# Layer 2 of the last five chunks by seven block products, and a written-out order for the last seven chunks

## The chip, the cores and the metric

The kernel runs on one core of one Trainium2 chip. The metric is device time in microseconds (us), the median of three runs. Engines: PE (matmuls), DVE, ACT and POOL (elementwise work), SP (issues nearly all DMAs).

## What is computed

Pooled attention, then a feed-forward block with a residual, on 8 batches x 576 tokens = 4608 tokens with 512 features:

```
k_p, v_p = mean of k, v over groups of 8 tokens          # 72 keys per batch, 8 heads of 64
attn = softmax(q @ k_p.T / 8);  x = attn @ v_p           # heads side by side: 4608 x 512
xn = (x - mean) / sqrt(var + 1e-6) * g_ln
out = x + max(xn @ w_ch1, 0) @ w_ch2                     # 512 -> 2048 -> 512
```

Inputs and output are float32. The kernel holds each factor of the feed-forward matmuls as a float16 main part and a float16 rest, and multiplies main x main, main x rest and rest x main: three matmuls for one product.

## The kernel before, in words

The tokens are cut into 36 tiles of 128 and 9 chunks of 512 (four tiles). Layer 1 gives for a chunk H = max(xn W1, 0), 2048 wide, in two halves (h = 0, 1) of 1024; layer 2 multiplies each half by its half of W2 and adds the result to x. Weights stay in SBUF as `wt[1]` and `wt[2]`, eight blocks each (and one spare), with main part and rest.

Layer 1 of chunks 2 to 8 works by seven products (Strassen's scheme in Winograd's form). The tokens of a chunk and the 512 features are cut in two each, and so are the features and the 1024 columns of a W1 half; seven products of blocks and of sums of blocks take the place of eight. `FACTOR` names them: A11, A12, A22 and S1 to S4 are blocks of z (the normalised x) and sums of them, B11, B21, B22 and T1 to T4 the same of W1. `product` (L807) runs six matmuls with 256 moving columns; `first_products`, `middle_products` and `last_product` bring the results from PSUM into a float32 buffer `cc` (ACT copies L835, L836, L842, L845; DVE additions L838, L844, L851), and then write H to `ring` as main part (ReLU on ACT, L857) and rest (DVE, L858). f = 0..3 counts the column blocks of a half: one f gives 2 x 128 columns of H for 512 tokens.

Layer 2, `ffn_out` (L870), is the plain product. For a half and a tile of 128 tokens it runs 24 matmuls with 512 moving columns (L882), weights from `ring`, moving columns from `wt[2]`. DVE adds the scaled result to x (L893), and after the second half SP writes the tile out (L898).

Attention for a later chunk runs between: `stage_a` (scores on PE L501, softmax on DVE, ACT and POOL L537, L540, then a DMA transpose L548) and `stage_b` (values on PE L633 and L634, statistics and z on DVE L681 and L698, the sums S1 to S4 L702 to L705, the split into main part on ACT L751 and rest on POOL L753, a DMA transpose L758). `prep_k` and `prep_v` load a batch's K and V and pool them on POOL (L371 to L375, L385 to L387).

Order of the work: chunks 0 and 1, all loading and preparing of weights, the sums T of W1 (`sums_w`, L339 to L347, L327) and attention up to tile 11 are written out by hand in the list START. A token names an operation, and each time it appears the operation goes on to its next `yield`; each engine gets its instructions in the order of the list. For chunks 2 to 8 the loop at the end of the kernel calls units one after the other, four of layer 1 and four of layer 2 for each half; `A_AT` and `B_AT` say before which unit a tile's attention stages stand, and a scheduler in the compiler then orders the instructions.

## Time and profile before

| what | value |
|---|---|
| median of three runs | 842.06 us (841.86 to 843.77) |
| the profiled execution | 842.33 us, its span 840.6 us |
| mean granted TensorE clock | 0.993 of full speed |
| PE, DVE, POOL, ACT busy | 96%, 65%, 41%, 40% of the span |
| first layer-1 product of chunk 2 | 242.9 us after the start of the span |
| last matmul ends | about 837 us |

How to read it: the span goes from the first to the last instruction of one execution; the time has about 2 us around it. "Busy" of PE is the union of its matmuls, which overlap one another, so the mean length of one (379 ns for 512 columns) is not what one costs in a row. In a group of instructions the columns are the source line, the engine, the operation, the output and inputs by their names, the shapes and the count, then busy us and mean ns, then how long the engine stood idle before them and for whom. A line of the chain gives its start, its length and the work in it.

### The profile page before, as it was taken

How to read it: one execution, taken by the hardware profiler on the slowest of the kernel's cores; microseconds unless marked ns; L12 is line 12 of the kernel's file. 1: busy time of each engine (PE TensorE's matmuls, PEld its weight loads, DVE VectorE, ACT ScalarE, POOL GpSimd, SP SyncE). 2: the span in 40 equal slices, each digit the busy share in tenths (PEclk: the TensorE clock that was granted, in tenths of full speed). 3: DMA queues.
4: the chain of work that ended last, by engine and by line, in shares of the span. 5: the costliest groups of instructions: out<-in, count | busy, mean ns of one | idle time of the engine just before them, and what ended most of it. 6: DMA issues, size and time to landing. Idle time of an engine off the chain costs nothing.

```text
span 840.6 us, 14847 instructions
## 1 busy us (share of the span) xinstructions
PE 809.4 (96%) x5742; PEld 527.5 (63%) x5742; DVE 545.3 (65%) x1110; ACT 339.1 (40%) x636; POOL 347.0 (41%) x497
## 2 busy tenths in 40 slices
...
GB/s 362 310 156 237 203 151 134 67 74 61 124 180 83 122 43 126 110 121 54 121 69 120 43 134 75 116 39 94 78 88 39 101 51 76 27 101 14 1 1 51
DMA packets 145975, 87.37 MB, mean 104 GB/s; under 512 B 125424, under 2 KB 126576, under 8 KB 143728
## 3 DMA queue, kind: packets, MB, share of 16 engines
...
q10 hardware_dynamic: 1152, 0.90, 0.5%
...
## 4 chain that ended last, share of the span: by engine, by line
PE 70%; DVE 10%; POOL 9%; DMA 4%; issue 3%; ACT 2%; ACTq 0%; SPq 0%; POOLq 0%; DVEq 0%
PE ps_f L882 34%; PE ps_f L817 25%; PE ps_f L784 5%; PE ps_a L501 3%; DMA vr<-in_v_dram 2%; POOL vr L385 2%; POOL vr L386 1%; DVE w L264 1%; POOL vp L387 1%; POOL kblk L375 1%; PE ps_m L441 1%; POOL pt L575 1%; PE ps_a L633 1%; DVE w L211 1%; PE ps_a L634 1%
## 5 line engine op out<-in xcount | busy, mean ns | idle before, releaser
L882 PE MATMUL ps_f<-w,ring 128*128 128x512 f16 x1728 | 380.7, 379 | 0.0
L882 PEld LDWEIGHTS <-ring 128*128 128x128 f16 x1728 | 167.7, 98 | 193.8 <-issue 0.2
L817 PE MATMUL ps_f<-zts,w 128*128 128x256 f16 x1680 | 209.0, 274 | 8.2 <-DVE rowmax L168 3.4
L817 PEld LDWEIGHTS <-w 128*128 128x128 f16 x1680 | 164.2, 98 | 30.1 <-issue 8.9
L893 DVE SCALAR_TENSOR_TENSOR x<-ps_f,cy,x 128x512 f32<-128x512 f32 x72 | 53.8, 748 | 114.4 <-PE ps_f L882 107.8
L537 POOL TENSOR_TENSOR phl<-e,phl 128x512 f16<-128x512 f32 x32 | 38.5, 1204 | 142.5 <-ACT phl L527 142.4
L817 PE MATMUL ps_f<-zts,tsp 128*128 128x256 f16 x672 | 96.1, 272 | 0.3 <-ACT raw L835 0.3
L784 PE MATMUL ps_f<-zts,w 128*128 128x512 f16 (+1 forms) x480 | 87.0, 340 | 3.2 <-DVE ring L795 2.4
L857 ACT ACTIVATE ring<-raw 128x512 f16<-128x512 f32 x112 | 64.8, 622 | 58.4 <-DVE raw L851 57.9
L858 DVE SCALAR_TENSOR_TENSOR ring<-raw,ring 128x512 f16<-128x512 f32 x112 | 81.6, 755 | 8.7 <-ACT ring L857 8.4
L835 ACT COPY raw<-ps_f 128x256 f32<-128x256 f32 x56 | 20.8, 371 | 138.2 <-PE ps_f L817 134.8
L753 POOL TENSOR_TENSOR hl<-raw,hl 128x640 f16<-128x640 f32 x28 | 41.4, 1495 | 81.4 <-ACT hl L751 45.6
L784 PEld LDWEIGHTS <-w 128*128 128x128 f16 x480 | 47.0, 99 | 40.0 <-issue 3.7
L817 PEld LDWEIGHTS <-tsp 128*128 128x128 f16 x672 | 64.0, 98 | 10.7 <-issue 0.5
L385 POOL TENSOR_TENSOR vr<-vr 72x256 f32<-72x256 f32 x56 | 50.0, 898 | 34.3 <-DMA vr<-in_v_dram 34.0
L851 DVE TENSOR_TENSOR raw<-ps_f,raw 128x256 f32<-128x256 f32 x112 | 42.3, 418 | 22.6 <-PE ps_f L817 22.6
L838 DVE TENSOR_TENSOR raw<-ps_f,raw 128x256 f32<-128x256 f32 x56 | 23.7, 424 | 48.4 <-PE ps_f L817 43.0
L844 DVE TENSOR_TENSOR raw<-ps_f,raw 128x256 f32<-128x256 f32 x56 | 23.5, 420 | 32.6 <-PE ps_f L817 27.4
L751 ACT CAST hl<-raw 128x640 f16<-128x640 f32 x28 | 19.2, 722 | 62.6 <-DVE a L728 26.3
L501 PE MATMUL ps_a<-kblk,q 128*128 128x144 f32 (+1 forms) x320 | 43.1, 288 | 0.9 <-DVE st L661 0.9
L501 PEld LDWEIGHTS ps_a<-kblk,q 128*128 128x128 f32 (+1 forms) x320 | 39.1, 179 | 6.4 <-issue 1.3
L753 POOL TENSOR_TENSOR hl<-z,hl 128x512 f16<-128x512 f32 x18 | 21.5, 1196 | 36.0 <-ACT hl L751 22.7
(144 smaller groups left out, 1002.9 us busy)
## 6 DMA issues: line engine op xcount, KB each, us to landing
...
```

The source lines that it names most:

```text
L385: eng.tensor_add(out=vr[:, 0:4, :], in0=vr[:, 0:4, :], in1=vr[:, 4:8, :])
L501: nc.tensor.matmul(ps[r, p // 2, p % 2 * 2 * KV : (p % 2 + 1) * 2 * KV], lhsT=q[:, p, r], rhs=kblk[b % NKB][:, p, :], start=True, stop=True,)
L537: nc.gpsimd.tensor_tensor(out=ph[:, 0, :, KA:P], in0=e[:, :, 0:KA], in1=ph[:, 0, :, 0:KA], op=ALU.subtract)
L753: nc.gpsimd.tensor_tensor(out=zhl[:, 1, :], in0=src, in1=zhl[:, 0, :], op=ALU.subtract)
L784: nc.tensor.matmul(ps, lhsT=w[:, part, fs], rhs=zT[:, kz, cols], start=(n == 0), stop=(n == 3 * NKT - 1),)
L817: nc.tensor.matmul(ps, lhsT=w[:, part, f * P : (f + 1) * P], rhs=z, start=start and n == 0, stop=stop and n == 3 * KH - 1, skip_group_chec ...
L838: nc.vector.tensor_tensor(out=cc[:, 0, :HC], in0=m2, in1=cc[:, 0, :HC], op=ALU.add)
L851: nc.vector.tensor_tensor(out=cc[:, j, HC:], in0=u3, in1=cc[:, j, HC:], op=ALU.add)
L857: nc.scalar.activation(out=hh[:, 0, f], in_=cc[:, j], func=AF.Relu)
L858: nc.vector.scalar_tensor_tensor(out=hh[:, 1, f], in0=cc[:, j], scalar=0.0, in1=hh[:, 0, f], op0=ALU.max, op1=ALU.subtract)
L882: nc.tensor.matmul(ps, lhsT=h[:, part, i, cols], rhs=w[:, wp, j], start=(n == 0), stop=(n == 3 * NFT // 2 - 1),)
L893: nc.vector.scalar_tensor_tensor(out=x, in0=ps, scalar=out_scale(c, tt, half), in1=x, op0=ALU.mult, op1=ALU.add)
```

## The change

Chunks 4 to 8 (c >= `C_TWO`) get layer 2 by seven products too. A half of H (512 tokens x 1024) is cut in two by tokens and in two by columns, the half of W2 (1024 x 512) in two by rows and by columns.

- *W2.* In chunks 2 and 3 `keep_w2` (KW) copies three blocks of each half of W2 to DRAM; `sums_w2` (TW, 16 steps) builds T1 to T4 in pieces of 128 columns (two DVE additions, four POOL subtractions, a split by ACT and POOL) and writes them to DRAM, two DMAs a step. From chunk 4 on `load_w2` (LW) reads one of the seven factors, 512 KB, for each product into one of four places in `ring`, which H no longer needs.
- *H.* `wt[2]` becomes the place of H's seven factors, one place each, and of the scratch `s_tmp`. For each f, EL makes A11 and A12 (ReLU and main part on ACT, rest on DVE), ER the ReLU of the other half of `cc` and A22, ES four sums on POOL, EP the split of S1 and S2 (i = 0) and of S3 and S4 (i = 1): main part on ACT, rest on POOL, for i = 0 in chunks 4 and 5 on DVE. `cc` has three buffers; the third is one of the two softmax buffers, which from tile 12 on is only one.
- *Products.* `out_seven` (O, c.h.n.u) runs 12 matmuls with 256 moving columns for one product n = 0..6 and one row tile u = 0, 1; three PSUM results per u gather them, and DVE adds each state that is final for a part of x into x. `W2_USE` gives the order n: A11, A12, A22, S1, S2, S4, S3.
- *Order.* The loop goes; STEADY, a list like START, orders every step of chunks 2 to 8. Layer 1 is `product` (P, c.h.f.m) with one eviction each, the seventh as one DVE instruction over 512 columns, and `whole_h` (WH) in chunks 2 and 3. z of chunks 3 to 8 is made on ACT.

The core of the diff:

```diff
+C_TWO = 4
-A_AT, B_AT = (0, 2, 5, 8), (4, 6, 11, 12)
+LO_GPSIMD = (6,7,8)
+STEADY = """
+P.2.0.0.2 TW.0.0.0 TW.0.0.0 A.12 HV.4.0 A.12 P.2.0.1.2 P.2.0.1.1 P.2.0.0.1 P.2.0.0.5 P.2.0.1.5 A.12 P.2.0.1.1 P.2.0.1.1
+P.2.0.0.1 P.2.0.0.1 A.12 A.12 TW.0.0.0 HV.4.0 HV.4.0 A.12 A.12 KW.1.1 KW.1.1 P.2.0.1.6 P.2.0.0.2 P.2.0.0.2 TW.0.0.1
...
+HV.7.1 HV.7.1 EP.6.0.3.1 EL.6.1.1 EP.6.0.3.1 EP.6.0.3.1 B.29 O.6.0.3.0 P.6.1.1.7 P.6.1.1.7 O.6.0.3.1 O.6.0.3.1
+O.6.0.3.0 O.6.0.3.0 EL.6.1.0 EL.6.1.0 B.30 O.6.0.4.1 O.6.0.4.1 ER.6.1.1 A.31 EP.6.1.0.0 A.31 ES.6.1.0 ES.6.1.0
+EP.6.1.0.0 EP.6.1.0.0 ES.6.1.1 A.31 A.31 B.29 B.29 O.6.0.5.1 O.6.0.6.0 O.6.0.6.1 P.6.1.2.1 O.6.0.5.1 O.6.0.5.1
+O.6.0.6.0 O.6.0.6.0 O.6.0.6.1 O.6.0.6.1 P.6.1.2.1 P.6.1.2.1 B.30 P.6.1.2.5 P.6.1.2.2 P.6.1.2.6 P.6.1.3.2 P.6.1.3.1
+P.6.1.2.2 P.6.1.2.2 B.30 B.30 P.6.1.2.5 P.6.1.2.5 O.6.0.5.0 P.6.1.2.4 B.31 O.6.0.5.0 O.6.0.5.0 B.31 P.6.1.2.6 P.6.1.2.6
+P.6.1.3.1 P.6.1.3.1 Z.30.0 EP.6.1.0.1 EP.6.1.1.0 P.6.1.2.4 P.6.1.2.4 EP.6.1.0.1 EP.6.1.0.1 ES.6.1.1 ES.6.1.1 Z.30.0
+Z.30.0 EP.6.1.1.0 EP.6.1.1.0 LW.6.1.1 LW.6.1.1 LW.6.1.0 LW.6.1.0 LW.6.1.2 LW.6.1.2 P.6.1.3.5 P.6.1.3.6 P.6.1.2.3
+P.6.1.2.3 P.6.1.2.3 P.6.1.3.2 P.6.1.3.2 P.6.1.3.5 P.6.1.3.5 Z.30.1 P.6.1.3.6 P.6.1.3.6 EP.6.1.1.1 EL.6.1.2 Z.30.1
...
-    ring = ctx.enter_context(tc.tile_pool(name="ring", bufs=2))
+    dram = ctx.enter_context(tc.tile_pool(name="dram", bufs=1, space=bass.MemoryType.DRAM))
...
+    ring = const.tile([P, 2, 2 * FPQ * CH], F16, name="ring")
...
-        ph = phl[t % 2]
+        ph = phl[t % 2 if t < 3 * TPC else 0]
...
-        (nc.gpsimd if c < 2 else nc.vector).tensor_scalar(
-            out=z, in0=x, scalar1=ln[:, 0:1], scalar2=ln[:, 2:3], op0=ALU.subtract, op1=ALU.mult
-        )
+        if c > 2:
+            nc.vector.scalar_tensor_tensor(
+                out=ln[:, 0:1], in0=ln[:, 0:1], scalar=-1.0, in1=ln[:, 2:3], op0=ALU.mult, op1=ALU.mult
+            )
+            yield
+            nc.scalar.activation(out=z, in_=x, func=AF.Identity, scale=ln[:, 2:3], bias=ln[:, 0:1])
+        else:
+            (nc.gpsimd if c < 2 else nc.vector).tensor_scalar(
+                out=z, in0=x, scalar1=ln[:, 0:1], scalar2=ln[:, 2:3], op0=ALU.subtract, op1=ALU.mult
+            )
         if not seven:
...
+    def left_buffer(c, h, f):
+        if "c" not in t_raw:
+            t_raw["c"] = t_raw.pop("t1").rearrange("p n c -> p (n c)").rearrange(
+                "p (i f c) -> p i f c", i=2, f=2
+            )
+        if c < C_TWO:
+            return t_raw["c"][:, f % 2]
+        if not C_BUF:
+            raw = phl[1].rearrange("p a h k -> p (a h k)").bitcast(F32).rearrange("p (i c) -> p i c", c=CH)
+            C_BUF.extend((t_raw["c"][:, 0], t_raw["c"][:, 1], raw))
+        return C_BUF[(2 * FPQ * c + FPQ * h + f) % 3]
+
+    def product(c, h, f, m):
+        if m in (1, 2, 5):
+            PS[c, h, f, m] = psum["ps_f"].tile([P, CH], F32, name="ps_f")
...
-                    start=start and n == 0,
-                    stop=stop and n == 3 * KH - 1,
+                    start=m in (1, 2, 4, 5) and n == 0,
+                    stop=m in (2, 3, 4, 7) and n == 3 * KH - 1,
...
+        j, k = divmod({1: 0, 2: 0, 3: 2, 4: 1, 5: 3, 6: 2, 7: 1}[m], 2)
+        o = cc[:, j, k * HC : (k + 1) * HC]
+        if m in (2, 3):
+            nc.vector.tensor_tensor(out=o, in0=ps, in1=o, op=ALU.add)
+        elif m == 7:
+            o = cc[:, :, HC:]
+            nc.vector.tensor_tensor(out=o, in0=ps.unsqueeze(1).broadcast_to([P, 2, HC]), in1=o, op=ALU.add)
+        else:
+            nc.scalar.copy(out=o, in_=ps)
...
+    def split_h(src, n, f, engine):
+        hi, lo = (wt[2][:, n, a, f * HC : (f + 1) * HC] for a in range(2))
+        nc.scalar.copy(out=hi, in_=src)
+        yield
+        engine.tensor_tensor(out=lo, in0=src, in1=hi, op=ALU.subtract)
+
+    def left_factors(c, h, f):
+        cc = left_buffer(c, h, f)[:, :, :HC]
+        nc.scalar.activation(out=cc, in_=cc, func=AF.Relu)
+        yield from split_h(cc, slice(0, 2), f, nc.vector)
+
+    def right_relu(c, h, f):
+        cc = left_buffer(c, h, f)
+        nc.scalar.activation(out=cc[:, :, HC:], in_=cc[:, :, HC:], func=AF.Relu)
+        yield from split_h(cc[:, 1:2, HC:], slice(2, 3), f, nc.vector)
+
+    s_tmp = wt[2][:, WB - 1].rearrange("p a n -> p (a n)").bitcast(F32).rearrange("p (i c) -> p i c", c=HC)
+
+    def right_sums(c, h, f):
+        cc = left_buffer(c, h, f)
+        r00, r01, r10, r11 = (cc[:, j, k * HC : (k + 1) * HC] for j in range(2) for k in range(2))
+        nc.gpsimd.tensor_tensor(out=s_tmp[:, 0], in0=r01, in1=r11, op=ALU.add)
+        nc.gpsimd.tensor_tensor(out=s_tmp[:, 1], in0=s_tmp[:, 0], in1=r00, op=ALU.subtract)
+        yield
+        nc.gpsimd.tensor_tensor(out=s_tmp[:, 3], in0=r10, in1=s_tmp[:, 1], op=ALU.subtract)
+        nc.gpsimd.tensor_tensor(out=s_tmp[:, 2], in0=r00, in1=r01, op=ALU.subtract)
+
+    def right_pair(c, h, f, i):
+        yield from split_h(s_tmp[:, 2 * i : 2 * i + 2], slice(3 + 2 * i, 5 + 2 * i), f, nc.gpsimd if i or c in LO_GPSIMD else nc.vector)
+
+    w2s = [dram.tile([7, P, FPQ // FPB, 2, FPB, HC], F16, name=f"w2s{h}") for h in range(2)]
+
+    def keep_w2(h, n):
+        i, j = ((0, 0), (1, 0), (1, 1))[n]
+        src = wt[2][:, 4 * h + 2 * i : 4 * h + 2 * i + 2].rearrange("p b a n -> p (b a n)")
+        src = src.rearrange("p (g n) -> p g n", n=CH)[:, :, j * HC : (j + 1) * HC]
+        nc.sync.dma_start(out=w2s[h][n].rearrange("p b a f n -> p (b a f) n"), in_=src)
+
+    def sums_w2(h, f, e):
+        flat = phl[1].rearrange("p a h k -> p (a h k)")
+        b = wk2.tile([P, POOL, KV], F32, name="kr").rearrange("p l k -> p (l k)")[:, : 4 * P]
+        b = b.rearrange("p (i c) -> p i c", c=P)
+        t = flat[:, e * 8 * P : (e + 1) * 8 * P].rearrange("p (i a c) -> p i a c", i=4, a=2)
+        for i in range(2):
+            src = wt[2][:, 4 * h + 2 * i + f // 2].rearrange("p a (f j c) -> p a f j c", f=FPB, j=4)[:, :, f % 2]
+            nc.vector.tensor_tensor(
+                out=b[:, 2 * i : 2 * i + 2], in0=src[:, 0, e::2], in1=src[:, 1, e::2], op=ALU.add
+            )
+        yield
+        b11, b12, b21, b22 = (b[:, i] for i in range(4))
+        nc.gpsimd.tensor_tensor(out=b11, in0=b12, in1=b11, op=ALU.subtract)
+        nc.gpsimd.tensor_tensor(out=b12, in0=b22, in1=b12, op=ALU.subtract)
+        yield
+        nc.gpsimd.tensor_tensor(out=b22, in0=b22, in1=b11, op=ALU.subtract)
+        nc.gpsimd.tensor_tensor(out=b21, in0=b21, in1=b22, op=ALU.subtract)
+        yield
+        nc.scalar.copy(out=t[:, :, 0], in_=b)
+        yield
+        nc.gpsimd.tensor_tensor(out=t[:, :, 1], in0=b, in1=t[:, :, 0], op=ALU.subtract)
+        yield
+        for a in range(2):
+            dst = w2s[h][W2_AT["T1"] : W2_AT["T1"] + 4, :, f // FPB, a, f % FPB, e * P : (e + 1) * P]
+            nc.sync.dma_start(out=dst.rearrange("i p c -> p i c"), in_=t[:, :, a])
+
+    W2_USE = (("A11", "B11"), ("A12", "B21"), ("A22", "T4"), ("S1", "T1"), ("S2", "T2"), ("S4", "B22"), ("S3", "T3"))
+    W2_AT = {n: i for i, n in enumerate(("B11", "B21", "B22", "T1", "T3", "T4", "T2"))}
+    H_AT = {n: i for i, n in enumerate(("A11", "A12", "A22", "S1", "S2", "S3", "S4"))}
+
+    def w2_buffer(c, h, n):
+        return ring.rearrange("p i (j b a f c) -> p (i j) b a f c", j=2, a=2, f=FPB, c=HC)[:, (14 * c + 7 * h + n) % 4]
+
+    def load_w2(c, h, n):
+        nc.sync.dma_start(out=w2_buffer(c, h, n), in_=w2s[h][W2_AT[W2_USE[n][1]]])
+
+    PO = {}
+
+    def out_seven(c, h, n, u):
+        left, b = H_AT[W2_USE[n][0]], w2_buffer(c, h, n)
+        if n in (0, 1, 3):
+            PO[c, h, u, n] = psum["ps_f"].tile([P, CH], F32, name="ps_f")
+        ps = PO[c, h, u, {0: 0, 1: 1, 2: 1, 3: 3, 4: 0, 5: 3, 6: 0}[n]][:, :HC]
+        for f in range(FPQ):
+            for part, wp in ((0, 0), (0, 1), (1, 0)):
+                nc.tensor.matmul(
+                    ps,
+                    lhsT=wt[2][:, left, part, f * HC + u * P : f * HC + (u + 1) * P],
+                    rhs=b[:, f // FPB, wp, f % FPB],
+                    start=n < 4 and f == 0 and part == wp == 0,
+                    stop=f == FPQ - 1 and part == 1,
+                    skip_group_check=True,
+                )
+        yield
+        tt = u + 2 * (n in (2, 3, 6))
+        t = c * TPC + tt
+        x, scale = X[t], out_scale(c, tt, h)
+        if n == 6:
+            x = x.rearrange("p (j c) -> p j c", j=2)
+            ps = ps.unsqueeze(1).broadcast_to([P, 2, HC])
+        else:
+            x = x[:, HC:] if n in (3, 4, 5) else x[:, :HC]
+        nc.vector.scalar_tensor_tensor(out=x, in0=ps, scalar=scale, in1=x, op0=ALU.mult, op1=ALU.add)
+        if h == 1 and n in (5, 6):
+            yield
+            nc.sync.dma_start(out=out[t * P : (t + 1) * P, :], in_=X.pop(t))
 
...
+    def run(tokens):
+        begun = {}
+        with tc.manual_schedule():
+            for token in tokens.split():
+                if token not in begun:
+                    name, *args = token.split(".")
+                    begun[token] = iter(ops[name](*map(int, args)) or ())
+                next(begun[token], None)
+            for steps in begun.values():
...
+    run(START)
...
-    for c in range(2, NRUN):
...
-            all_of(op(*args))
+    run(STEADY)
```

368 lines of the change are left out of this document (293 added, 75 removed).

## The prediction

> **What bounds the kernel now.** I read the page's first part, then the windows cut at the first layer-1 product of each chunk (chunk 2 starts at 242.9 us, chunk 8 ends at 837.0), then the chain in order of time, then the groups by form.
>
> ```profile
> PE 809.4 (96%) x5742; PEld 527.5 (63%) x5742; DVE 545.3 (65%) x1110; ACT 339.1 (40%) x636; POOL 347.0 (41%) x497
> ```
>
> ```profile
> 242.90:330.20 87.30, 85.12 (x627) 57.15 (x627) 53.48 (x122) 30.16 (x64) 44.43 (x79) 0.98 0.45 106
> 330.20:417.20 87.00, 84.37 (x628) 57.89 (x627) 54.78 (x123) 31.44 (x67) 36.43 (x60) 1.00 0.44 99
> 417.20:503.50 86.30, 86.30 (x658) 58.84 (x657) 56.58 (x119) 31.59 (x67) 31.89 (x51) 1.00 0.37 92
> 503.50:589.60 86.10, 83.78 (x621) 56.99 (x619) 55.39 (x122) 31.17 (x67) 23.34 (x37) 1.00 0.37 85
> 589.60:674.60 85.00, 85.00 (x651) 57.97 (x650) 52.33 (x112) 30.70 (x66) 15.39 (x18) 1.00 0.32 72
> 674.60:758.76 84.16, 84.16 (x627) 57.77 (x626) 52.31 (x112) 30.67 (x66) 13.95 (x14) 1.00 0.32 64
> 758.76:837.00 78.24, 78.12 (x528) 51.41 (x526) 28.92 (x57) 20.24 (x48) 0.00 (x0) 1.00 0.04 14
> 837.00:840.60 3.60, 0.00 (x0) 0.00 (x0) 0.67 (x1) 0.00 (x0) 0.00 (x0) 0.90 0.19 73
> ```
>
> The columns behind the length are busy us of PE, weight loads, DVE, ACT and POOL, then granted clock, DMA share and GB/s. In chunks 2 to 8 (one row each) PE is busy 586.85 of 594.10 us: it is the bound, at full clock, with 7.25 us of idle to win. DVE stands at 61 to 66% until chunk 7, ACT at 35 to 37%, and POOL falls from 51% to 17%. Busy time alone does not say that PE works at its best rate, so I take rates from unbroken runs on the chain:
>
> ```profile
> 174.16 20.72 PE ps_f L882 x96
> 758.76 16.38 PE ps_f L817 x150
> 779.47 18.35 PE ps_f L882 x85
> 836.91 0.75 DVE x L893
> ```
>
> 96 matmuls with 512 moving columns take 20.72 us, 215.8 ns each; 150 with 256 columns take 16.38, 109.2 ns each. The narrow form costs 0.506 of the wide one.
>
> **The change part by part.** *Layer 2 of chunks 4 to 8.* Before, a chunk has 2 halves x 4 token tiles x 24 = 192 wide matmuls: 41.43 us. After, it has 2 halves x 7 products x 2 row tiles x 12 = 336 narrow ones: 36.69 us. That is 4.74 us a chunk, **23.7 us** for five, all on the path. Layer 1, attention and layer 2 of chunks 2 and 3 keep their matmuls.
>
> [...]
>
> *The floor.* The first 242.9 us keep their list, and the load of the first stage changes nothing but where a buffer lies. 242.9 + 586.85 - 23.7 = 806.05; with the 3.60 us behind the last matmul and the 842.33 - 840.60 = 1.73 us that the profiled execution has beside its span, a PE without any idle gives 811.4. (Its 842.33 is 0.27 above the median of 842.06, well inside the 0.3%, 2.5 us, that can be told from no change here.)
>
> *What a fixed list leaves idle.* The stage before is run from such a list already:
>
> ```profile
> 120.00:160.00 40.00, 40.00 (x209) 19.59 (x207) 30.05 (x52) 16.37 (x25) 33.93 (x37) 1.00 0.48 121
> 160.00:200.00 40.00, 40.00 (x187) 18.16 (x186) 25.05 (x39) 9.69 (x17) 31.43 (x45) 1.00 0.22 54
> 200.00:242.90 42.90, 41.55 (x267) 21.54 (x265) 33.86 (x76) 14.93 (x25) 25.78 (x39) 1.00 0.52 124
> ```
>
> PE idles 1.35 of 122.9 us, 1.1%, beside a POOL that is 74% busy. On 563 us that is 6.2 us; it takes the place of the 7.25.
>
> *The new elementwise work,* by these rows:
>
> ```profile
> L858 DVE SCALAR_TENSOR_TENSOR ring<-raw,ring 128x512 f16<-128x512 f32 x112 | 81.6, 755 | 8.7 <-ACT ring L857 8.4
> L857 ACT ACTIVATE ring<-raw 128x512 f16<-128x512 f32 x112 | 64.8, 622 | 58.4 <-DVE raw L851 57.9
> L893 DVE SCALAR_TENSOR_TENSOR x<-ps_f,cy,x 128x512 f32<-128x512 f32 x72 | 53.8, 748 | 114.4 <-PE ps_f L882 107.8 <-PE ps_m L191 3.9 <-PE ps_f L191 1.8
> L838 DVE TENSOR_TENSOR raw<-ps_f,raw 128x256 f32<-128x256 f32 x56 | 23.7, 424 | 48.4 <-PE ps_f L817 43.0 <-ACT raw L835 5.1
> L753 POOL TENSOR_TENSOR hl<-raw,hl 128x640 f16<-128x640 f32 x28 | 41.4, 1495 | 81.4 <-ACT hl L751 45.6 <-issue 35.9
> L339 DVE TENSOR_TENSOR raw<-w 128x512 f32<-128x512 f16 x16 | 15.4, 1018 | 0.0
> ```
>
> ```profile
> L385 POOL TENSOR_TENSOR vr<-vr x56: 714/723/1782, 28.5 to 505.3; 72x256 f32<-72x256 f32 x56
> L753 POOL TENSOR_TENSOR hl<-raw,hl x28: 1390/1400/1851, 227.0 to 750.3; 128x640 f16<-128x640 f32 x28
> L753 POOL TENSOR_TENSOR hl<-z,hl x18: 1148/1155/1905, 119.7 to 711.1; 128x512 f16<-128x512 f32 x18
> L341 POOL TENSOR_TENSOR raw<-raw x4: 1274/1646/1652, 120.8 to 186.7; 128x512 f32<-128x512 f32 x4
> ```
>
> For each of a chunk's 8 column blocks of H:
> - ACT loses two splits (L857) and gains two ReLUs, the A11/A12 split, the half-width A22 split and two splits of sums: about 5.4 instructions for 2, +3.4 x 0.62 = 2.1 us. It also makes the normalised z, six instructions of about 0.62. Per chunk +17 +4 = 21 us: ACT at 52 of 80. If the new Identity function needs a table of its own, two loads at 1.28 each of the six times are 15 us, which the 28 left still cover:
>
> ```profile
> L446 ACT ACT_TABLE_LOAD x1 | 1.3, 1283 | 0.8 <-PEq L1029 0.8
> ```
>
> - DVE loses L858 twice (1.4) and gains rests of 0.7 and 0.42 (in chunks 4 and 5 another 0.7). Each half has 12 evictions at 0.42 and two at 0.75 where four at 0.75 were: +7.1 a chunk, while z leaves it (about -3). DVE lands near 54 to 62 of 80.
> - POOL gains four sums at 0.72 (L385) and one rest at 1.16 (L753; two in chunks 6 to 8): 4.0 or 5.2 us, 32 or 42 a chunk. Chunk 4: 31.9 + 32 = 64 of 80, chunk 7: 14 + 42 = 56.
> - Chunks 2 and 3 get 8 steps each of W2 sums: DVE 2 x 0.5 (half of L339), four POOL sums of 128 columns, at most 0.72 each, a split: 4.0 us of POOL, 32 a chunk. Chunk 2: 44.4 + 32 = 76 of 84.5, the fullest stage of any engine but PE. Nobody but the later loads waits for these sums.
>
> Attention and K/V steps keep their instructions and engines (K/V of batch 4 in chunk 2, of 7 until chunk 6), so their shares stand in the rows already. By sums all of this lies beside PE and costs nothing. By order it need not: H's parts have one place each, so POOL may start the S parts of a half only behind the last layer-2 product of the half before, and PE needs them all before its S4 and S3 products. In chunk 6 the list has for PE between those two points ten layer-2 products (12 x 109.2 = 1.31 us, 13.1), ten layer-1 products (6.6) and three attention steps (about 3.0: chunk 7's 84.16 less 78.12 is 6.0 for eight): 22.7 us. For POOL it has seven rests (8.1), five half steps of sums (7.2), four z rests of 640 columns (5.6): 20.9, and the first waits for an ACT split of 0.62. Slack 1 us in 22.7. Counted likewise the second halves of chunks 4, 5, 7, 8 have 0, 3, 0 and 5 us, first halves 2 to 16 (chunk 4's, at the turn from the old scheme, is 4 short unless some of it runs early). L753's mean stands 7% over its median where others do not get in its way: 7% of some 22 us is 1.5 us a half, minus what slack there is. I put **4 us** for the nine boundaries: 0 if the medians hold, 14 if every half loses its 1.5.
>
> [...]
>
> *Loads.* 70 loads of 512 KB come in, in SP's queue, with the transposes and q loads behind each one that waits for its slot; the waiting one holds back attention's transposes, two tiles ahead of their use. Rows:
>
> ```profile
> 0.00:40.00 40.00, 29.64 (x230) 22.65 (x230) 29.20 (x53) 25.63 (x33) 19.02 (x31) 1.00 0.94 351
> ```
>
> ```profile
> 502.53 2.66 DMA vr<-in_v_dram
> ```
>
> At 351 GB/s a load takes 1.5 us of all 16 engines, 14 a chunk 21 us: DMA share 0.37 + 0.26. 144 KB landed 2.66 us after issue; 368 KB more at that rate make 3.7, as an estimate, between 2.7 and, behind another load, 5.2. The tightest is the fifth of each half: its slot is free when the first product has run, and it is used two to three products of 2.6 us later, 4.9 us in chunk 6. It fits at 3.7; at 5.2 it costs 0.3 us in ten halves, 3 us. I take 0. The W2 sums leave in 256-byte runs in chunks 2 and 3 and are read tens of us later: nothing, or 2 us once if the first load comes too early.
>
> *Tail.* Four outputs of 256 KB instead of one follow in the last 5 us: 0.75 MB at 351 GB/s is 2.1 us more, partly under the last products: +1.
>
> Sum: 811.4 + 6.2 + 4 + 1 = 822.6, say **822**.
>
> **The rivals.** *POOL sets the end (slower).* The price of a POOL instruction decides. L341's row shows 1646 where 1274 was possible, a factor of 1.29. At that factor the windows, of 15 to 42 us of POOL work, overrun PE by 8, 3, 6, 6 and 0 us in the second halves and by 16, 3, 8, 4 and 0 in the first: 54 us, and 811.4 + 54 + 1 = 866. It turns slower from a factor of about 1.19, where the overruns make 30. For it: no slack in three halves. Against it: medians at the minima while DVE ran at 65%, and a cheap change of engine:
>
> ```profile
> 809.63 1.15 ACT L857 ACTIVATE ring<-raw 128x512 f16<-128x512 f32 x2 [1.58 <-DVE raw L851]
> 810.29 1.29 DVE L858 SCALAR_TENSOR_TENSOR ring<-raw,ring 128x512 f16<-128x512 f32 x2 [0.37 <-ACT ring L857]
> ```
>
> The first of two ACT instructions of 0.62 ends at 810.25 and DVE starts at 810.29; six such changes a half, ten halves, are 2.4 us, inside the 4 above. Chance 0.08.
>
> *Half of it given back.* Waits of 1.5 us at each boundary (14), late loads (3) and the chunk-2/3 stage, where POOL at 76 of 84.5 delays attention by up to 4: 811.4 + 6.2 + 14 + 3 + 4 + 1 = 840, no more than just faster. Between that and the forecast lie all mixtures. Chance of ending within 0.3% of before: 0.05; of 828 to 839.5, where only some of these come: 0.22.
>
> *The narrow rate is not reached.* If the new products, whose weights were just written by ACT, DVE and POOL, ran above 123 ns (215.8 x 192 / 336) the swap would lose. Layer 1 has run 2352 such matmuls on fresh z, and 150 in a row show 109.2; were it a fifth slower, five chunks would take 13 us more than before, 811.4 + 23.7 + 13 + 11 = 859. Chance 0.01. [...]
>
> *The list runs as in the stage before and no boundary loses:* 811.4 to 818. Chance 0.2.
>
> **How the numbers follow.** Forecast case, 818 to 828: 0.44. The range of 8 in 10 leaves 0.03 below and 0.17 above (0.03 of the mixtures and all that isn't faster): 812 to 837. Faster by over 0.3% is 0.20 + 0.44 + 0.22 = 0.86; within it 0.05; slower 0.08 + 0.01 = 0.09.
>
> **What would show it.** PE instructions: 5 x (336 - 192) = 720 more, 6462. A run of layer-2 products at 109.2 ns. Chunks 4 to 7 near 81 us, chunk 8 near 74 to 76, chunks 2 and 3 near 85. Idle of PE ahead of S products, if any, released by POOL rests. I am wrong if these chunks stay near 85, if a chunk's POOL share nears 95%, or if weight loads or DMA head the idle time of PE.

## The result, and the profile after

The changed kernel takes 829.05 us (median of 4 runs, 828.21 to 831.16), the kernel before 842.74 beside it (4 runs, 841.86 to 843.77): a ratio of 0.9846, 95% interval 0.9817 to 0.9875. The profiled execution took 828.21, 1.7 of it outside its span. The forecast was 822, the range 812 to 837: faster as said, but some 7 us of the 20 foreseen did not come.

The first part of the page, with engines, share of the span and instruction counts:

```profile
PE 788.9 (95%) x6462; PEld 595.7 (72%) x6462; DVE 635.1 (77%) x1190; ACT 456.4 (55%) x848; POOL 605.4 (73%) x801
```

The 720 additional matmuls are there. POOL's busy time is what the prediction's prices give: 347.0 + 2 x 32 (chunks 4, 5) + 3 x 42 (6 to 8) + 2 x 32 (sums of W2) = 601, measured 605. DVE's is not: by those prices 5 x (7.1 - 3) + 16 (sums of W2) = 36 us come in (the rests that change hands, 11 us less in chunks 4 to 8 and 11 more in chunks 4 and 5, cancel), and the profile shows 90 more than before.

The windows, cut where a chunk's last layer-2 step begins (in the list the first products of a chunk run before that), so a row is one chunk, 2 to 8; columns as in the prediction:

```profile
239.85:325.32 85.47, 84.09 (x670) 58.94 (x670) 71.22 (x143) 42.86 (x86) 64.84 (x104) 1.00 0.56 130
325.32:411.24 85.92, 84.83 (x627) 57.28 (x626) 63.82 (x117) 40.73 (x82) 67.45 (x106) 1.00 0.63 154
411.24:504.85 93.61, 89.22 (x831) 75.99 (x829) 78.69 (x146) 53.47 (x109) 72.43 (x101) 0.98 0.66 182
504.85:592.11 87.26, 84.54 (x798) 75.04 (x796) 75.20 (x146) 53.28 (x109) 68.62 (x93) 1.00 0.65 176
592.11:672.73 80.62, 77.80 (x765) 68.78 (x763) 62.37 (x117) 49.77 (x99) 58.99 (x67) 1.00 0.62 169
672.73:748.61 75.88, 74.62 (x725) 66.72 (x722) 58.09 (x116) 48.33 (x98) 56.15 (x63) 1.00 0.56 152
748.61:822.03 73.42, 73.04 (x668) 64.97 (x665) 40.75 (x79) 36.65 (x79) 43.12 (x48) 1.00 0.35 118
```

Chunks 4 and 5 are the fullest on every engine, and there PE's busy time misses the length by 4.4 and 2.7 us; chunk 6 misses 2.8 and chunk 8 0.4. Chunk 4 is also the one row whose granted clock is below 1.00. An unbroken run of layer-2 products from the chain in order of time:

```profile
803.62 7.87 PE ps_f L1236 x72
```

It is 109.3 ns a matmul, on weights that ACT, DVE and POOL had just written: layer 1's 109.2 holds here.

Busy time still hides short waits, since matmuls overlap: a narrow one of L1236 lasts 274 ns on average and starts 109 behind the one before it. So I count what PE *loses*: from the first layer-1 product to the end of the last matmul (its start and its rate), less all matmuls at the rates of their unbroken runs. In the changed kernel that is 822.03 - 239.85 = 582.18 us, less 4032 narrow ones at 109.2 ns (440.3), 384 wide ones at 215.8 (82.9) and some 38.5 for the attention's 652: **20.5 us lost**. For the kernel before the same count is 836.7 - 242.9 = 593.8 less 582.4 (561.7 + 23.7 - 3.0, below), **11.4** lost (its busy time showed 7.25). The difference of the two executions is then: -23.7 from the swap, +9.1 lost, +0.6 behind the last matmul, together -14.0 of the 14.1 seen. That the first product starts 3.05 us earlier is no gain: the scores of three tiles, 24 matmuls, came before it and now come after.

One part of the lost time is no wait. Behind the first product each of the two kernels has one stretch of 3.4 us in which the granted clock is half (third number from the end); the first row is the changed kernel, the second the one before:

```profile
480.30:483.70 3.40, 3.26 (x16) 2.33 (x17) 3.33 (x7) 2.54 (x6) 3.01 (x4) 0.51 0.25 78
```

```profile
246.00:249.40 3.40, 3.40 (x18) 2.35 (x17) 0.42 (x1) 2.57 (x5) 1.08 (x3) 0.50 0.92 308
```

Narrow matmuls start 213 ns apart there instead of 109, and some 1.6 us are lost, in both kernels alike. In the changed kernel the stretch follows right behind three stops of PE in chunk 4's second half that add up to 2.2 us. no_pool_rest, below, has the same three (2.27 us) and no stretch. What decides is not shown, so the table below counts the half clock by itself.

Where PE waits, in the words of the waits view (us in total, times, longest):

```profile
PEld L1236 <- DVE w L1157: 9.9, 10, 1.6
PE ps_f L1236 <- DVE w L1157: 7.1, 9, 1.4
PE ps_f L1236 <- DVE x L1253: 2.3, 4, 0.8
PEld L1236 <- DMA ring<-w2s: 0.3, 1, 0.3
```

L1236 is layer 2 by seven products, L1157 the rests of H's factors, L1253 the evictions. No row has layer 2 wait for POOL. The waits lie at a few places: in the second halves of chunks 4, 5 and 6, where layer 2 starts, PE loses 2.34, 1.98 and 2.27 us. In chunk 4 the next 12 matmuls take 1.25 us more, by the half clock and not by a wait, and 1.53 us are lost ahead of the first S product, at 491.76, again for a rest on DVE.

What DVE does at the first of them (its rows of the timeline, then POOL's for the same 5.5 us):

```profile
472.51 0.69 DVE L1157 TENSOR_TENSOR w<-w 128x512 f16<-128x512 f32 x1
473.12 0.42 DVE L1133 TENSOR_TENSOR phl<-ps_f,phl 128x256 f32<-128x256 f32 x1
473.45 4.56 DVE L1157 TENSOR_TENSOR w<-raw,w 128x512 f16<-128x512 f32 x1
477.93 0.41 DVE L1133 TENSOR_TENSOR raw<-ps_f,raw 128x256 f32<-128x256 f32 x1
478.27 0.14 DVE L940 SCALAR_TENSOR_TENSOR ln<-ln 128x1 f32<-128x1 f32 x1
```

```profile
473.34 0.72 POOL L1177 TENSOR_TENSOR w<-raw,w 128x256 f32<-128x256 f32 x1
474.02 0.72 POOL L1178 TENSOR_TENSOR w<-raw 128x256 f32<-128x256 f32 x1
474.71 2.75 POOL L1044 TENSOR_TENSOR hl<-raw,hl 128x640 f16<-128x640 f32 x2
```

A rest of the same form takes 0.69 us at 472.51 and 4.56 at 473.45. The long one begins while POOL works and ends 0.55 us after POOL's last instruction in a row. POOL's four take their usual time (two sums, two z rests). The short one began 0.05 us ahead of POOL's next instruction, and there POOL's is the long one: 0.82 us (L645), where most of that line take 0.32. The group rows by form (the left rests, then a step on four elements) say how general that is:

```profile
L1157 DVE TENSOR_TENSOR w<-raw,w 128x512 f16<-128x512 f32 x26 | 28.0, 1078 | 3.2 <-ACT w L1155 3.1
L1157 DVE TENSOR_TENSOR w<-phl,w 128x512 f16<-128x512 f32 x14 | 13.6, 969 | 1.0 <-ACT w L1155 0.9
L996 DVE TENSOR_SCALAR y<-ve 128x4 int32<-128x4 int32 x9 | 4.9, 549 | 0.3
```

The 40 left rests cost 41.6 us, not 40 x 0.68 = 27.2. Added up over every DVE instruction behind the first product, the time above the shortest one of its line and shape is 104 us, against 38 before: of DVE's 90 us more, some 66 are such stretching, not work.

### The profile page after: what moved, and what is told of

It reads as the page before. It is cut to its first block, busy times and chain, and to the rows that moved or that the text cites. A ratio compares the mean times of both kernels' runs of the same rounds, so it can differ in the third digit from the quotient of the medians.

```text
span 826.5 us, 17098 instructions
## 1 busy us (share of the span) xinstructions
PE 788.9 (95%) x6462; PEld 595.7 (72%) x6462; DVE 635.1 (77%) x1190; ACT 456.4 (55%) x848; POOL 605.4 (73%) x801
## 4 chain that ended last, share of the span: by engine, by line
PE 68%; DVE 19%; POOL 6%; DMA 2%; issue 2%; ACT 2%; ACTq 0%; DVEq 0%; POOLq 0%
PE ps_f L1119 24%; PE ps_f L1270 16%; PE ps_f L1236 16%; PE ps_f L1075 7%; DVE w L1157 4%; PE ps_a L759 2%; DVE w L522 1%; DVE x L1253 1%; PE ps_a L891 1%; PE ps_a L892 1%; POOL vr L643 1%; POOL pt L833 1%; DVE w L469 1%; PE ps_m L699 1%; DVE raw L1136 1%
## 5 line engine op out<-in xcount | busy, mean ns | idle before, releaser
L1236 PE MATMUL ps_f<-ring,w 128*128 128x256 f16 x1680 | 196.3, 274 | 9.5 <-DVE w L1157 7.1
L1236 PEld LDWEIGHTS <-w 128*128 128x128 f16 x1680 | 163.7, 98 | 33.0 <-DVE w L1157 9.9
L1119 PEld LDWEIGHTS <-w 128*128 128x128 f16 x1680 | 163.6, 98 | 22.2 <-issue 1.8
L1270 PE MATMUL ps_f<-w,ring 128*128 128x512 f16 x768 | 169.5, 379 | 1.4 <-DVE ring L1149 1.4
L1270 PEld LDWEIGHTS <-ring 128*128 128x128 f16 x768 | 74.3, 98 | 89.6 <-DVE ring L1149 4.0
L1138 ACT COPY raw<-ps_f 128x256 f32<-128x256 f32 x168 | 60.2, 372 | 100.4 <-PE ps_f L1119 93.3
L1157 POOL TENSOR_TENSOR w<-w 128x512 f16<-128x512 f32 x64 | 77.1, 1209 | 28.0 <-ACT w L1155 22.8
L1075 PEld LDWEIGHTS <-w 128*128 128x128 f16 x480 | 47.3, 100 | 40.2 <-issue 3.8
L1155 ACT CAST w<-w 128x512 f16<-128x512 f32 x80 | 48.8, 618 | 40.4 <-POOL w L1175 15.1
L1253 DVE SCALAR_TENSOR_TENSOR x<-ps_f,y,x 128x256 f32<-128x256 f32 (+1 forms) x70 | 34.4, 516 | 28.3 <-PE ps_f L1236 27.9
L1157 DVE TENSOR_TENSOR w<-raw,w 128x512 f16<-128x512 f32 (+1 forms) x52 | 47.1, 914 | 6.4 <-ACT w L1155 6.3
L1253 DVE SCALAR_TENSOR_TENSOR x<-ps_f,cy,x 128x256 f32<-128x256 f32 (+1 forms) x70 | 35.1, 516 | 17.5 <-PE ps_f L1236 16.9
L1133 DVE TENSOR_TENSOR raw<-ps_f,raw 128x256 f32<-128x256 f32 x84 | 34.3, 415 | 15.8 <-ACT raw L1138 8.3
```

The lines of the kernel that those rows point to most:

```text
L1075: nc.tensor.matmul(ps, lhsT=w[:, part, fs], rhs=zT[:, kz, cols], start=(n == 0), stop=(n == 3 * NKT - 1),)
L1119: nc.tensor.matmul(ps, lhsT=w[:, part, f * P : (f + 1) * P], rhs=z, start=m in (1, 2, 4, 5) and n == 0, stop=m in (2, 3, 4, 7) and n == 3 ...
L1138: nc.scalar.copy(out=o, in_=ps)
L1155: nc.scalar.copy(out=hi, in_=src)
L1157: engine.tensor_tensor(out=lo, in0=src, in1=hi, op=ALU.subtract)
L1236: nc.tensor.matmul(ps, lhsT=wt[2][:, left, part, f * HC + u * P : f * HC + (u + 1) * P], rhs=b[:, f // FPB, wp, f % FPB], start=n < 4 and ...
```

## The theories and the experiments

*Theory A:* the late engine is DVE, because its instructions that work on SBUF alone are held while POOL works. *Theory B* (the prediction's): POOL's sums and rests are late. *Theory C:* DVE is late by the amount and order of its work, nothing is held. *Theory D:* the loads of W2. The table gives PE's lost us, counted as above from each run's profile (pieces of a chunk's half are cut at its last layer-2 step, "a" and "b" are halves); the last column is the part of them lost at half clock. The time is the median; no_el_rest, no_pool_rest, el_psum and one_tile ran once each, the changed kernel four times, over 3.0 us. Where the list is the same, a piece repeats within some 0.1 us in most cases.

| run | time | 2, 3 | 4a | 4b | 5a | 5b | 6a | 6b | 7, 8 | all | half clock |
|---|---|---|---|---|---|---|---|---|---|---|---|
| changed | 829.05 | 3.6 | 1.6 | 5.4 | 1.3 | 2.4 | 0.5 | 3.3 | 2.4 | 20.5 | 1.6 |
| no_el_rest | 818.13 | 3.7 | 1.0 | 1.8 | 0.0 | 0.7 | 0.1 | 1.3 | 1.1 | 9.6 | 0 |
| no_pool_rest | 818.30 | 3.9 | 0.3 | 3.6 | 0.3 | 2.0 | 0.1 | 0.1 | -0.1 | 10.1 | 0 |
| el_psum | 823.77 | 4.5 | 0.3 | 4.0 | 0.0 | 1.3 | 0.1 | 2.2 | 2.1 | 14.4 | 0 |
| one_tile | 828.16 | 3.6 | 1.5 | 5.4 | 1.3 | 2.4 | 0.5 | 3.4 | 2.2 | 20.2 | 1.7 |
| el_early | 828.34 | 3.7 | 1.6 | 6.4 | 1.3 | 2.6 | 0.5 | 1.7 | 2.2 | 20.0 | 1.5 |
| el_6 | 827.57 | 4.0 | 1.6 | 5.4 | 1.3 | 2.4 | 0.5 | 1.6 | 2.2 | 19.0 | 1.7 |
| z_late | 833.41 | 4.0 | 1.6 | 6.8 | 1.3 | 3.9 | 0.5 | 2.5 | 2.3 | 22.8 | 1.6 |
| pool_4 | 833.52 | 4.5 | 1.6 | 12.1 | 1.3 | 2.4 | 0.5 | 1.6 | 2.3 | 26.3 | 3.5 |
| lo_dve | 831.62 | 4.0 | 1.6 | 5.4 | 1.3 | 2.5 | 1.2 | 3.1 | 4.1 | 23.2 | 1.6 |
| lo_pool | 845.50 | 4.1 | 6.8 | 9.6 | 4.6 | 4.3 | 0.5 | 3.3 | 2.2 | 35.4 | 5.4 |

**The two engines side by side.** A kernel of its own, 24 instructions in a row of each kind.

```
for ops in ((dve_rest,), (pool_rest,), (pool_sum,), (pool_one,), (dve_psum,), (dve_small,), (dve_one,),
            (dve_rest, pool_rest), (dve_rest, pool_sum), (dve_rest, pool_one),
            (dve_psum, pool_rest), (dve_small, pool_rest), (dve_one, pool_rest), (act_one, pool_rest)):
    for op in ops:
        for _ in range(24): op()
    fence()
```

> Not the computation: 24 instructions of each of several kinds, first alone, then VectorE's or ScalarE's 24 beside GpSimd's 24, each stage closed before the next. Theory A: GpSimd's instructions last as long as alone (1.16 us the rest of 512, 0.72 the sum of 256); VectorE's rest of 512, 0.68 us alone, lasts about as long as GpSimd's instruction beside it or more (1.2 to 2.4 us), and so does VectorE's small scale of 4 elements (0.16 alone, about 1.2 beside); VectorE's sum that reads PSUM keeps its 0.41 us. The prediction's view: GpSimd's rest is stretched to 1.4 to 1.9 us beside VectorE's and VectorE's keeps 0.68.

Groups by form, in the windows of the single stages. DVE's rest and its small scale alone, POOL's rest alone:

```profile
L388 DVE TENSOR_TENSOR dlo<-cc,ch 128x512 f16<-128x512 f32 x24 | 16.6, 692 | 0.8
```

```profile
L394 DVE TENSOR_SCALAR ty<-ve 128x4 f32<-128x4 f32 x24 | 4.1, 170 | 0.8
```

```profile
L400 POOL TENSOR_TENSOR slo<-sp,sh 128x512 f16<-128x512 f32 x24 | 27.6, 1151 | 3.6 <-DVE ao L385 1.8
```

Beside one another: rest and rest, then DVE's addition from PSUM, DVE's small scale and ACT's split, each beside POOL's rest:

```profile
L400 POOL TENSOR_TENSOR slo<-sp,sh 128x512 f16<-128x512 f32 x24 | 35.8, 1490 | 3.7 <-DVE slo L385 1.9
L388 DVE TENSOR_TENSOR dlo<-cc,ch 128x512 f16<-128x512 f32 x24 | 35.7, 1489 | 0.8
```

```profile
L400 POOL TENSOR_TENSOR slo<-sp,sh 128x512 f16<-128x512 f32 x24 | 27.6, 1152 | 3.6 <-DVE ao L385 1.8
L391 DVE TENSOR_TENSOR ds<-pp,cc 128x256 f32<-128x256 f32 x24 | 10.2, 424 | 0.8
```

```profile
L400 POOL TENSOR_TENSOR slo<-sp,sh 128x512 f16<-128x512 f32 x24 | 27.7, 1156 | 3.6 <-DVE slo L385 1.8
L394 DVE TENSOR_SCALAR ty<-ve 128x4 f32<-128x4 f32 x24 | 14.2, 591 | 0.8
```

```profile
L400 POOL TENSOR_TENSOR slo<-sp,sh 128x512 f16<-128x512 f32 x24 | 27.7, 1152 | 3.6 <-DVE ao L385 1.8
L409 ACT CAST ao<-ac 128x512 f16<-128x512 f32 x24 | 14.8, 618 | 415.2 <-DVE ao L385 414.4
```

Two streams of rests beside one another run at 1.49 us a pair. DVE's is stretched from 0.69 by 115%, POOL's from 1.15 by 29%. So theory A is right on DVE and the prediction's view on POOL (1.4 to 1.9 us), each wrong on the other engine. DVE's addition from PSUM takes 0.424 us beside POOL's rest and 0.424 alone; ACT's split takes 0.618, on average what it takes in the changed kernel (L1155, 0.605 to 0.642); and POOL's rest keeps its 1.15 beside either. A scale of four elements is stretched on average from 0.17 to 0.59. A pair costs 1.49, where one after the other would be 0.69 + 1.15 = 1.84, while the 4.56 us rest above lasted until four of POOL's instructions were done; what decides between the two isn't shown here.

**Rests that read PSUM, and the control.** The 40 left rests keep their place and size, only the wide operand lies elsewhere.

```diff
-        yield from split_h(cc, slice(0, 2), f, nc.vector)
+        hi, lo = (wt[2][:, 0:2, a, f * HC : (f + 1) * HC] for a in range(2))
+        nc.scalar.copy(out=hi, in_=cc)
+        yield
...
+        same = pa[0][:, :, 512 - P :].unsqueeze(2).broadcast_to([P, 2, 2, P])
+        nc.vector.tensor_tensor(out=lo, in0=same, in1=hi, op=ALU.subtract)
```

> VectorE's 40 rests of the left factors stay in number, size and place, but their wide operand is read from a spare part of the scores' PSUM tile instead of SBUF (so the remainder that they write is not A11's and A12's); the scores and values share that one tile throughout. GpSimd's work stays. Theory A (held because two operands lie in SBUF): the rests take 0.70 us whatever GpSimd runs, the long ones of 1.2 to 4.6 us are gone, TensorE's waits for them at the second halves fall from 9 us to under 3, and the time falls by 5 to 9 us, to 820 to 824. Theory C (the amount of VectorE's work and its place): nothing moves, 828 to 831. Theory B: the waits go over to GpSimd's rests, 827 to 829.

The control keeps that tile (made once behind the START list) and lets the rests read SBUF:

```diff
+    pa.append(psum["ps_a"].tile([P, 2, 512], F32, name="ps_a"))
+    nc.vector.memset(pa[0][:, :, 512 - P :], 0.0)
...
-        ps = psum["ps_s"].tile([P, 2, 512], F32, name="ps_a")
+        ps = pa[0] if pa else psum["ps_s"].tile([P, 2, 512], F32, name="ps_a")
```

> The control of el_psum: scores and values share one PSUM tile as there, and the left rests read SBUF as in the changed kernel. If the gain of el_psum came from where the rests read, this one is back at 828 to 831 us with 20 us of idle time; if it came from the shared tile, it is near 824.

In el_psum, first the group, then the same place in the timeline (DVE, then POOL):

```profile
L1169 DVE TENSOR_TENSOR w<-ps_a,w 128x512 f16<-128x512 f32 x40 | 27.0, 683 | 8.7 <-PE ps_a L761 3.1 <-PE ps_a L894 2.8 <-ACT w L1165 2.6
```

```profile
474.69 0.68 DVE L1169 TENSOR_TENSOR w<-ps_a,w 128x512 f16<-128x512 f32 x1
476.20 0.42 DVE L1135 TENSOR_TENSOR raw<-ps_f,raw 128x256 f32<-128x256 f32 x1 [0.83 <-PE ps_f L1121]
476.54 2.19 DVE L942 SCALAR_TENSOR_TENSOR ln<-ln 128x1 f32<-128x1 f32 x1
```

```profile
474.58 0.72 POOL L1184 TENSOR_TENSOR w<-raw,w 128x256 f32<-128x256 f32 x1
475.26 0.72 POOL L1185 TENSOR_TENSOR w<-raw 128x256 f32<-128x256 f32 x1
475.95 2.76 POOL L1046 TENSOR_TENSOR hl<-raw,hl 128x640 f16<-128x640 f32 x2
```

Beside the first two of the same four POOL instructions the rest that took 4.56 us takes 0.68; the next DVE instruction with SBUF inputs, one element wide, takes 2.19 beside the other two, one that took 0.14 when POOL was done in the changed kernel. The time is 823.77, the lost time 14.4; with the shared tile alone it is 828.16 and 20.2. Of these 5.8 us, 1.7 are the stretch at half clock, which el_psum does not have. So some 4 of the 20.5 us are the holding of these 40 rests, with DVE's and POOL's work and order unchanged; whether the half clock goes with it is open. PE's waits for DVE's rests fall from 7.1 us to 4.4, not under 3: 1.9 for the left ones, and 2.5 ahead of chunk 4's first S product, for a rest that still reads SBUF. The two times are one execution each; what carries the reading is the mean of 683 ns and the places. For these rests theory A is shown, and theory C, which had nothing move, is refuted as the whole cause.

**Leaving one side's rests out.**

```diff
-        yield from split_h(cc, slice(0, 2), f, nc.vector)
+        nc.scalar.copy(out=wt[2][:, 0:2, 0, f * HC : (f + 1) * HC], in_=cc)
+        yield
```

> Leaves out VectorE's 40 rests of the left factors in layer 2 of chunks 4 to 8 (the f16 remainder of A11 and A12 is stale). Theory A and theory C: TensorE's 9 us behind VectorE's rests fall under 2 us and the time falls by 6 to 9 us, to 820 to 823. Theory B: TensorE then waits as long for GpSimd's sums and rests, and the time falls by 0 to 2 us. Theory D: 829 us.

```diff
-        engine.tensor_tensor(out=lo, in0=src, in1=hi, op=ALU.subtract)
+        if engine is not nc.gpsimd:
+            engine.tensor_tensor(out=lo, in0=src, in1=hi, op=ALU.subtract)
```

> Leaves out GpSimd's 64 rests of the right factors' sums (the f16 remainder of most S parts is stale), 64 times 1.16 = 74 us of GpSimd's work; VectorE's work and its order stay. Theory A: VectorE's rests are held less, the mean of its left rests falls from 0.8 to about 0.73 us, and TensorE's 9 us behind them fall to 4 to 6, the time by 3 to 6 us to 823 to 826. Theory B: the waits at the second halves go altogether, 819 to 822 us. Theory C: TensorE's 9 us behind VectorE's rests stay, and the time falls by 0 to 2 us, what TensorE waits for GpSimd.

Both save 11 us (818.13 and 818.30), more than any theory gave; for no_pool_rest theory B's 819 to 822 comes nearest. Neither has the stretch at half clock, which is 1.6 of the 11. Without DVE's left rests the losses at the three places vanish. Without POOL's rests those of chunks 4 and 5 stay (2.27 and 1.98 us at the start of layer 2), against theory B: there POOL runs z rests, which this kernel keeps, and PE still waits for DVE's rests (4.6 us in six waits, where the changed kernel has 7.1 in nine). Chunk 4's half falls from 5.4 to 3.6 by the half clock, hardly by its waits. Chunk 6, where S rests stood beside them, falls from 3.3 to 0.1. Relieving either engine was worth the same.

**Other orders.** el_early moves DVE's steps, z_late POOL's z rests, away from the three places.

```diff
-... P.6.1.2.7 P.6.1.2.7 EL.6.1.1 EL.6.1.1 EL.6.1.2 EL.6.1.2 B.31 EL.6.1.3 ER.6.1.2 P.6.1.3.4 P.6.1.3.4 B.31 ... EL.6.1.3 EL.6.1.3 ER.6.1.2
+... EL.6.1.1 B.31 P.6.1.2.6 ... P.6.1.2.7 P.6.1.2.7 EL.6.1.1 EL.6.1.2 EL.6.1.2 EL.6.1.3 ... EL.6.1.3 EL.6.1.3 B.31 B.31 ER.6.1.2
```

> Only the list changes: the rest of left factor 1 goes ahead of the attention scores' statistics in the second halves of chunks 4, 5 and 6, the statistics' next step goes behind the rest of left factor 3 in chunks 4 and 6, and the first step of chunk 3's token scales goes behind the last hidden rest of chunk 2. Theory A (VectorE is the late engine at the second halves, because its instructions on SBUF alone are held while GpSimd works): the 9 us that TensorE waits there for VectorE's rests shrink by 3 to 5 us, 824 to 826 us. Theory B (the prediction's: GpSimd's sums and rests are late): nothing moves, 829 us within 0.5. Theory C (VectorE's work and its order alone, nothing held): the gain is 2 to 3 us, since only what was queued ahead counts. Theory D (the loads of W2's sums): no change.

The time is 828.34 (ratio to before 0.9837, 0.9799 to 0.9874): nothing that can be told from the changed kernel. In chunk 4 the left rest indeed ran earlier, and in its place a rest of S1 and S2 that DVE makes there was held for 4.68 us by the same four POOL instructions, so the half lost 1.0 more. Only chunk 6 gained, 1.6 us.

> The part of el_early that helped there, alone: in the second half of chunk 6 the rest of left factor 1 goes ahead of the scores' second step, and the statistics' last steps go behind the rest of left factor 3. In el_early the idle time in that half was 1.65 us where it was 3.29 in the changed kernel, and in chunk 4 it was 1.0 us more, so that this list should give 1.5 to 2 us: 827 to 827.5 us.

el_6 is the edit shown, alone: 827.57 us (0.9819, 0.9791 to 0.9846), lost 19.0. The profile shows the 1.6 us in chunk 6; the medians alone can't tell it from the changed kernel. It has the lowest median of the lists in this study.

```diff
-... Z.22.0 Z.22.0 Z.22.1 Z.22.1 HV.7.0 ... XT.22.0 XT.22.0 XT.22.1 XT.22.1 A.25 EL.4.1.3 EL.4.1.3
+... HV.7.0 ... A.25 EL.4.1.3 EL.4.1.3 Z.22.0 Z.22.0 Z.22.1 Z.22.1 XT.22.0 XT.22.0 XT.22.1 XT.22.1
```

> Only the list changes, and in it only GpSimd's rests of the normalised rows (parts Z.22.0, Z.22.1, Z.26.0 and Z.30.1) and their transposes: they go behind the rest of left factor 3 in the second halves of chunks 4, 5 and 6; VectorE's own order stays. Theory A in its sharper form (VectorE's left rests are held there by the 1.4 to 1.9 us z rests that GpSimd runs beside them): the idle time at the start of layer 2 in these halves, 7.8 us, falls to 3 or 4, and the time by 3 to 5 us, to 824 to 826. Theory C (VectorE's amount of work and its order alone): no change, 828 to 830. A third view (GpSimd always has something else to run, and whatever it is holds VectorE as long): the waits move to the next step and the time changes by under 1 us.

833.41 us, 4 slower instead of 3 to 5 faster (0.9898, 0.987 to 0.9925). At the start of layer 2 it did what was expected: chunk 4's 2.34 us vanished, chunk 5's 1.98 became 0.77, chunk 6's 2.27 became 1.61. But it came back later in the same halves: ahead of chunk 4's first S product PE loses 2.5 us where 1.5 were, the stretch at half clock comes at 495.7, and loads are late. A row of SP's queue between 470 and 520 us, and two of PE's waits in the whole of z_late:

```profile
SPq L1032 <- POOL hl L1041: 9.0, 2, 6.6
```

```profile
PE ps_f L1233 <- DMA ring<-w2s: 4.9, 3, 2.4
PE ps_f L1233 <- DVE w L1154: 2.6, 5, 0.7
```

The transposes that follow the moved rests (L1032) stand in SP's queue until POOL is done, and behind them stand the loads of W2's sums, for which layer 2 now waits 4.9 us, once each in chunks 4, 5 and 6. I had moved the steps without counting what they queue.

```diff
-... HV.7.0 ES.4.1.1 HV.7.0 B.21 B.21 B.20 B.20 HK.6.1 ... HV.7.0 ES.4.1.1 ES.4.1.1 Z.22.0
+... ES.4.1.1 B.21 B.21 B.20 B.20 ... ES.4.1.1 ES.4.1.1 Z.22.0 ... EP.4.1.3.1 EP.4.1.3.1 HV.7.0 HV.7.0 HK.6.1 HK.6.1 ... P.5.0.0.1 P.5.0.0.1 HV.7.0 HV.7.0
```

> The list of el_6, and besides it the pooling of K and V for later batches (GpSimd's steps of HV.7.0 and HK.6.1, some 5 us) goes out of the first part of chunk 4's second half, behind the last sums of that half; the work stays. If VectorE's left rests and GpSimd's sums are both late there for what GpSimd runs ahead of them, the idle time of that half falls from 5.4 us to 2 to 4 and the time to 824 to 826 us. If only the order on VectorE counts, it stays at el_6's 827.6.

pool_4 does the same with the pooling of K and V, and fails the same way: 833.52 us (0.9896, 0.9871 to 0.9921). The loss at the start of chunk 4's second half is gone; a load of V (L634) now waits on SP for POOL, 8.1 us, and the last load of W2's sums goes out 0.42 us behind it, at 498.94:

```profile
498.52 0.32 SPq L634 DMA_DIRECT2D vr<-in_v_dram  x1
498.94 0.34 SPq L1222 DMA_DIRECT2D ring<-w2s  x1
```

PE loses 5.7 us for it. It also loses 2.7 us instead of 1.5 ahead of chunk 4's first S product, and the granted clock is at half behind that stop, and again in and behind the one for the load: 10.2 us in all, for 3.5 us of loss. Theory D is no cause in the changed kernel (0.3 us), but it stands right behind.

**Work from one engine to the other.** LO_GPSIMD names the chunks whose first S rests run on POOL: (6, 7, 8) in the changed kernel, none in lo_dve, (4, 5, 6, 7, 8) in lo_pool.

```diff
-LO_GPSIMD = (6,7,8)
+LO_GPSIMD = (4,5,6,7,8)
```

> The 24 first rests of the right sums in chunks 6 to 8 go from GpSimd (1.16 us each, 28 us) to VectorE (0.69 each, 17 us and what holds them). Theory B (GpSimd late): 3 to 5 us faster. Theory C (VectorE's work alone): 2 to 4 us slower. Theory A: GpSimd's instruction that held VectorE for up to 1.16 us is replaced with one of 0.69 on VectorE itself, so between 2 us faster and 1 us slower.

> The 16 first rests of the right sums in chunks 4 and 5 go from VectorE (0.69 us each, 11 us) to GpSimd (1.16 each, 19 us). Theory B: 1 to 3 us slower. Theory C: 1 to 3 us faster, the waits at chunks 4 and 5 shrinking. Theory A: between 1 us faster and 2 us slower.

lo_dve takes 831.62 (0.9882, 0.9851 to 0.9913), lo_pool 845.50 (1.0039, 1.0019 to 1.0060). lo_dve's 2.6 us more lie in theory C's range and not in A's, though its interval overlaps the changed kernel's. All theories missed lo_pool's size: 16 rests on POOL, 19 us of its work, cost 16 us of time. In lo_pool PE waits for POOL:

```profile
PE ps_f L1236 <- POOL w L1157: 11.7, 4, 4.1
PE ps_f L1236 <- DVE w L1157: 6.5, 7, 1.4
```

So theory B is not wrong about how close POOL is: at chunks 4 and 5 it has no slack, and of 19 us more work some 12 come out as waits of PE. Another 3.8 us of the loss are half clock, 13.6 us long in three stretches where the changed kernel has one of 3.4. In the changed kernel POOL is simply not the engine that ends last. Moving 28 us away from POOL in chunks 6 to 8 doesn't help either: 17 of them come back on DVE.

**The order without the swap.** The list of the change with whole hidden tiles and plain layer 2 in chunks 4 to 8, in the places of the new steps.

```diff
-EL.c.h.f ER.c.h.f ES.c.h.f EP.c.h.f.i LW.c.h.n O.c.h.n.u  (c = 4..8)  KW TW
+WH.c.h.f  G.c.tt.h
```

> The fixed list without the new layer 2: in chunks 4 to 8 the seven products' steps of layer 2, the right and left factors, the loads and the kept sums of W2 are out, and whole hidden tiles and the plain layer 2 of 4 tiles a half are in their places; the rest of the list keeps its order. By the prediction's sum the plain layer 2 gives back 23.7 us of TensorE, and the idle time of the list would be under 20 us: 838 to 846 us, so that the order alone is worth between a loss of 4 and a gain of 4 us. If the gain came from the fixed order, it would be near 829.

850.51 us (1.0096, 1.006 to 1.0131), 4.5 above the expected range; lost 20.7. The page's first line has the 720 fewer matmuls:

```profile
PE 812.0 (95%) x5742; PEld 526.4 (62%) x5742; DVE 510.5 (60%) x1042; ACT 364.8 (43%) x672; POOL 346.3 (41%) x497
```

From its first product to its last matmul it takes 606.1 us, the changed kernel 582.2: 23.9 apart at equal losses. That is no second measurement of the swap's 23.7, since the losses are counted at the same rates; and the losses are equal by luck, for they lie elsewhere: here layer 1 waits 5.4 us for ACT's copies (`raw`, L1045), and 2.8 are half clock. This list was derived, not tuned, and says nothing of what a tuned order without the swap would take; it does say that this order by itself brought no gain.

## Why the prediction was right and wrong

- *The swap, 23.7 us:* right, by 720 more matmuls and 109.3 ns in the run of 72.
- *The floor, 811.4:* in effect right. The first product comes 3.05 us earlier with 3 us more work behind it.
- *Idle of the fixed list, 6.2 us:* the step used busy time, which had hidden 4 us of the kernel before, some 1.6 of them half clock and the rest short waits; they were inside its 586.85, so the sum did not suffer. In the two chunks with the old layer 2 the list loses 3.6 us, mostly where DVE's rest of H (L1149) is late: its median is 0.88 us and its longest 1.88, where the shortest takes 0.68.
- *4 us for the boundaries, by POOL:* **the step that failed.** The losses do lie mostly at the second halves of chunks 4 to 6 (11.1 us; 2.4 in 7 and 8 together), but the releasing engine is DVE, and chunks 4 to 8 lose 16.9 us, 1.6 of them by half clock, which the sum had no term for. By the count used here the forecast had 14.4 in all (6.2 + 4 and the hidden 4.1); 20.5 came, which is the 6 us between 822.6 and 828.2. The measured time lies in the band from 828 to 839.5, which had a chance of 0.22; but the losses named for it were waits for POOL, late loads and chunks 2 and 3, so the number is in the range and the account of the losses is not right.
- *The rests at 0.7 and 0.42 on DVE:* this price lay beneath it. Rows of before gave it beside a POOL that was busy 17 to 51% of a chunk; at 59 to 79% (chunks 4 to 8) the 40 left rests average 1.04 (41.6 / 40), DVE is busy for 78.7 and 75.2 us of chunks 4 and 5 where 54 to 62 a chunk were put, and el_psum against its control shows some 4 us for the holding of these alone. The prediction looked for stretched instructions only in POOL's rows, on the side that is stretched less (29% against 115% in side_by_side). Its own trace had the other side:

```profile
L698 DVE TENSOR_SCALAR raw<-x,ln x14: 535/544/3011, 224.0 to 741.0; 128x512 f32<-128x512 f32 x14
```

  The instruction of 3.01 us, at 487.39, (z of a tile) ran beside five of POOL in a row (486.77 to 490.58); the median of its line is 0.54.
- *POOL's slack of 0 to 1 us:* near, as lo_pool shows for chunks 4 and 5. POOL's price of 1.16 us nearly held (its rests average 1.21), while DVE was held instead.
- *POOL sets the end, 866:* did not happen; with 19 us more on POOL it is 845.5.
- *Loads at nothing:* right, 0.3 us; z_late and pool_4 show 4.9 and 5.5 us of waits as soon as something on SP waits longer ahead of them.
- *Tail +1:* 4.47 us behind the last matmul, 3.9 before by the same reading: +0.6, near.
- *Signs named beforehand:* 6462 matmuls, narrow rate, chunk 8 at 73.4 for 74 to 76: seen, or near. Chunks 4 to 7 at 81: the mean of the rows is 84.3, from 93.6 down to 75.9, which is near the 85 that was named as a sign of being wrong, with chunks 4 and 5 above it. "Idle ahead of S products, released by POOL rests": seen once, in chunk 4, but released by DVE's rest.

What stays open: of the 11 us that leaving out DVE's left rests saves, some 4 are holding of these and 1.6 are half clock; how the other 5 divide between their plain work and holding of other DVE instructions was not measured, nor what brings the half clock on.
